# Swapping the side that carries the stride: activations that reorder tokens write SBUF in order and read PSUM strided

## The chip, the cores and the metric

The kernel runs on one core of a Trainium2 chip. The metric is device time in microseconds (us). A time is the median of several executions; different calls may run on different chips, so each comparison below is made with executions of the kernel before on the same chip, and a ratio compares the fast runs of the two kernels from the same rounds, as the measuring program worked it out. That is not quite the ratio of the medians quoted beside it. Profiles are single executions. Their span is about 2 us shorter than the device time of the same execution.

Engines in the profile: PE is the matrix engine (PEld its weight loads), ACT is ScalarE, DVE is VectorE, POOL is GpSimd, SP is SyncE.

## The reference

Two layers follow one another. The first is attention over 4 batches, 8 heads, 768 tokens and head size 64. A query sees the first 8 keys ("global") and the last 96 ("local"), with a bias that falls linearly with distance. The second takes the 3072 token rows of 512 values, sends each to one of 8 experts (top 1), or skips it, and adds the result:

```python
def _attn_ref(q, k, v, n_global, n_local):          # (4, 8, 768, 64), 8, 96
    scores = scale * np.matmul(q, k.transpose(0, 1, 3, 2))
    ...                                             # keep = is_global | is_local, plus bias
    a = np.exp(scores - max);  a = a / a.sum()
    return np.matmul(a, v)

def _moe_ref(x, w_skip, w_gate, w1, w2):            # x: (3072, 512)
    do_compute = x @ w_skip > 0
    e_idx = np.argmax(x[do_compute] @ w_gate, axis=1)
    ...
        h = np.maximum(xc[mask] @ w1[e], 0.0)
        y[mask] = gate_w[mask, None] * (h @ w2[e])
    out[do_compute] = xc + y
```

## The kernel before

Attention runs over 16 head pairs (a batch and two heads). q and k are loaded with eight neighbouring tokens in one SBUF partition: token `8p + r` sits in partition `p` (0 to 95) at place `r` (0 to 7). Transposing such a tile gives tokens in the order `(r, p)`. The kernel wants them back in the order `(p, r)`, which is the natural one, so the ScalarE instruction that moves a result from PSUM to SBUF also reorders it. In the kernel before, that instruction reads PSUM in order and writes SBUF with the stride: neighbouring elements of the stream land 8 bf16, that is 16 bytes, apart.

```python
# R = 8, P = 96, S = 768, W = 224
# transposes(n, 1): keys, PSUM (bf16) -> kt
kt = t_pool.tile([128, S], BF16, tag="kt", name="kt")
nc.scalar.activation(out=kt[:, :].rearrange("a (p r) -> a r p", r=R), in_=ps[:, :, :],
                     func=ACT.Copy)

# global_scores(b): scores against the global keys, PSUM (fp32) -> g_sb
nc.scalar.activation(
    out=g_sb[:, u * (S // 2):(u + 1) * (S // 2)].rearrange("a (p r) -> a r p", r=R),
    in_=gp[:, :, :], func=ACT.Exp, bias=gbias[:, 0:1], scale=scale)

# scores(n, g): local scores of two key tiles and two heads, PSUM (fp32) -> a
sc = ps_sc.tile([128, 2, 512], FP32, tag="sc", name="sc")
...                                        # matmuls write sc[:, hh, kk*W : ...] in order (r, p)
nc.scalar.activation(
    out=a[:, :, :].rearrange("a h (k p r) -> a h k r p", k=2, r=R),
    in_=sc[:, :, 0:2 * W].rearrange("a h (k r p) -> a h k r p", k=2, r=R),
    func=ACT.Exp, scale=scale)
...                                        # the last of three groups: two smaller activations
nc.vector.tensor_tensor(out=a[:, :, 0:wid], in0=a[:, :, 0:wid], in1=m[:, :, 0:wid], op=ALU.mult)
```

The loads of q, k and v are issued by GpSimd, and so are the small copies `kg` of the first keys of each head, which the global scores need:

```python
def load_v(b, ones=True):
    vb = v_pool.tile([128, T, H, D1], BF16, tag="vb", name="vb")
    for t in range(T):
        nc.gpsimd.dma_start(out=vb[:, t, :, 0:D], in_=v_r[b, t])
    nc.gpsimd.memset(vb[:, :, :, D:D1], 1.0)       # a column of ones beside v
    vbs[b] = vb

def keys_global(n):
    ...
        nc.gpsimd.tensor_copy(out=kg[b % 2][...], in_=kts[n][..., 0:KG])
```

After attention come the last gate, then a gather of each expert's tokens, the late weights (three of eight experts; the other five are loaded during attention), the experts' matmuls and the scatter of their results.

The softmax here doesn't subtract the row's maximum and nothing guards it: scores larger than these inputs give would overflow.

## Time and profile before

| | before |
|---|---|
| time, median of 3 (later 4) executions | 416.79 us (416.69) |
| ScalarE busy | 282.1 us, 68% of the span |
| matmul busy | 176.9 us, 43% |
| VectorE busy | 105.0 us, 25% |
| issue of the experts' first gather, start of the tail | 312.2 us |

From the page of the kernel before: the span, and each engine's busy us, share of the span and number of instructions.

```profile
span 414.9 us, 4722 instructions
...
PE 176.9 (43%) x1869; PEld 127.0 (31%) x1877; DVE 105.0 (25%) x311; ACT 282.1 (68%) x144; POOL 122.5 (30%) x183
...
```

The trace lacks eight matmul records: PE shows 1869 instructions here and 1877 in the other full traces.

The busy-by-stretch view cuts the run into stages; shown are the loop over the 16 head pairs and the tail. Its columns are the stretch, its length, each engine's busy us with its number of instructions, the granted clock of PE, the packet time of the DMA engines as a share of 16 of them (it can exceed 1) and GB/s.

```profile
...
46.00:297.00 251.00, 98.64 (x1209) 72.68 (x1208) 66.93 (x196) 219.91 (x89) 44.15 (x81) 0.81 0.52 76
312.00:415.00 103.00, 64.36 (x441) 43.03 (x449) 17.70 (x29) 19.02 (x32) 60.56 (x62) 0.81 0.61 144
...
```

In the loop, 46 to 297 us, ScalarE is busy 219.9 of 251 us. A head pair takes 251 / 16 = 15.7 us. In the tail it is busy 19 of 103. So only a saving in the loop and the start can pay through ScalarE.

Which instructions are they? The groups by form, ScalarE only (busy us, then mean ns of one):

```profile
...
L286 ACT ACTIVATE a<-sc 128x896 bf16<-128x896 f32 x32 | 133.9, 4436 | 4.6 <-PE sc L281 4.6
L245 ACT ACTIVATE kt<-tr 128x768 bf16<-128x768 bf16 x16 | 61.7, 3858 | 0.9 <-PE tr L237 0.9
L293 ACT ACTIVATE a<-sc 128x448 bf16<-128x448 f32 x16 | 37.1, 2316 | 0.0
L293 ACT ACTIVATE a<-sc 128x256 bf16<-128x256 f32 x16 | 26.2, 1640 | 0.0
L580 ACT ACTIVATE ht<-hps 128x512 bf16<-128x512 f32 x32 | 19.0, 597 | 64.9 <-PE hps L577 64.9
L264 ACT ACTIVATE g_sb<-gp,gbias 128x384 bf16<-128x384 f32 x8 | 14.7, 2081 | 16.0 <-PE gp L261 16.0
...
```

The first, second, third, fourth and sixth of these lines are the five forms that reorder. Together they record 133.9 + 61.7 + 37.1 + 26.2 + 14.7 = 273.6 us. The fifth, `ht`, does not reorder: 512 elements in 597 ns. An 896-element reorder takes 4436 ns, 7.4 times as long for 1.75 times the elements. Records of neighbouring instructions overlap a little; the chain of waits gives the net pace:

```profile
...
12.09 8.09 ACT a L286 x2
...
```

Two of them back to back take 8.09 us, which is 4.5 ns per element.

### The profile page before, as it was taken

Reading aid. Unit: us, or ns where it says so; the run is one execution under the profiler, and the core shown is the slowest. Engines: PE = TensorE matmul, PEld = TensorE weight load, DVE = VectorE, ACT = ScalarE, POOL = GpSimd, SP = SyncE. Lnnn points to the kernel's source line nnn. Section 1 sums busy time; section 2 is a strip of 40 time slices with the busy share of each in tenths; the row PEclk is TensorE's granted clock in tenths of the full one; section 3 lists DMA queues with packets and bytes.
Section 4 is the critical chain, followed back from the end, with each engine's and each line's share of the span. In section 5 each row is a group of like instructions: output and inputs, shape, how many; then the busy total and the mean of one; then the engine's idle time right before and its main releaser. Section 6 shows DMA issues by size and latency. Waiting matters only on the chain.

```text
span 414.9 us, 4722 instructions
## 1 busy us (share of the span) xinstructions
PE 176.9 (43%) x1869; PEld 127.0 (31%) x1877; DVE 105.0 (25%) x311; ACT 282.1 (68%) x144; POOL 122.5 (30%) x183
## 2 busy tenths in 40 slices
PE   1201643243344332424335150534533898399700
PEld 1101332232133332312324140323522575176400
DVE  5112122213111133241212233113761120232200
ACT  7999799999799996949999785898010232033200
POOL 8240642115101241010520000000007545477770
PEclk9999999999999999999555555656555899699965
DMA  8950792209402192040499997000204999544430
GB/s 117 125 76 2 92 63 38 38 2 114 114 2 38 17 98 39 0 114 2 68 203 212 212 212 183 0 2 0 77 0 88 231 230 199 173 130 136 128 96 15
DMA packets 50520, 38.24 MB, mean 92 GB/s; under 512 B 30276, under 2 KB 39492, under 8 KB 50496
## 3 DMA queue, kind: packets, MB, share of 16 engines
q0 software_dynamic: 45568, 34.62, 52.5%
q1 hardware_dynamic: 4928, 3.30, 2.8%
q8 instruction: 16, 0.26, 0.2%
q14 instruction: 8, 0.07, 0.1%
HBM read 54.68 MB, written 13.63 MB: 165 GB/s over the span
## 4 chain that ended last, share of the span: by engine, by line
ACT 43%; issue 21%; PE 13%; DMA 9%; DVE 9%; POOL 3%; POOLq 0%; ACTq 0%; DVEq 0%
ACT a L286 14%; ACT kt L245 12%; ACT a L293 12%; PE yps L584 4%; PE hps L577 3%; DMA w<-in_moe_w_dram 3%; DMA xg<-x_rows,src 3%; DMA out_dram<-y,rows 3%; ACT xts L360 2%; ACT g_sb L264 2%; POOL xg L545 1%; DVE xb L330 1%; PE gp L261 1%; PE sc L281 1%; ACT mask L161 1%
## 5 line engine op out<-in xcount | busy, mean ns | idle before, releaser
L286 ACT ACTIVATE a<-sc 128x896 bf16<-128x896 f32 x32 | 133.9, 4436 | 4.6 <-PE sc L281 4.6
L299 DVE TENSOR_TENSOR a<-a,mask 128x896 bf16<-128x896 bf16 (+1 forms) x48 | 28.7, 597 | 193.5 <-ACT a L286 106.0
L580 ACT ACTIVATE ht<-hps 128x512 bf16<-128x512 f32 x32 | 19.0, 597 | 64.9 <-PE hps L577 64.9
L245 ACT ACTIVATE kt<-tr 128x768 bf16<-128x768 bf16 x16 | 61.7, 3858 | 0.9 <-PE tr L237 0.9
L281 PE MATMUL sc<-qt,kt 64*128 64x224 bf16 x192 | 24.6, 354 | 81.3 <-ACT a L286 45.8
L293 ACT ACTIVATE a<-sc 128x448 bf16<-128x448 f32 (+1 forms) x32 | 55.1, 1978 | 0.0
L253 POOL COPY kg<-kt 64x16 bf16<-64x16 bf16 x32 | 6.1, 192 | 158.0 <-ACT kt L245 157.2
L545 POOL DMA_INDIRECT xg<-x_rows,src x16 | 15.7, 980 | 73.8 <-DVE gate L537 60.1
L281 PEld LDWEIGHTS <-kt 64*128 64x128 bf16 x192 | 9.4, 107 | 88.1 <-issue 72.6
L584 PE MATMUL yps<-w,ht 128*128 128x512 bf16 x120 | 29.2, 394 | 8.0 <-DVE y L589 7.6
L577 PE MATMUL hps<-xt,w 128*128 128x256 bf16 x256 | 31.4, 284 | 0.0
L237 PE MATMUL tr<-ident,qr 96*64 96x96 bf16 x256 | 13.6, 280 | 35.6 <-ACT kt L245 34.5
L554 POOL DMA_INDIRECT out_dram<-xb,skip_k x24 | 24.1, 1004 | 13.2 <-DMA w<-in_moe_w_dram 6.5
L577 PEld LDWEIGHTS <-w 128*128 128x128 bf16 x256 | 25.8, 102 | 4.1
L317 PE MATMUL av<-vb,a 128*128 128x65 bf16 x192 | 26.4, 243 | 0.0
L589 DVE SCALAR_TENSOR_TENSOR y<-yps,gate,xg 128x512 f32<-128x512 f32 x16 | 11.9, 750 | 54.4 <-PE yps L584 29.0
L264 ACT ACTIVATE g_sb<-gp,gbias 128x384 bf16<-128x384 f32 x8 | 14.7, 2081 | 16.0 <-PE gp L261 16.0
L324 PE MATMUL av<-vb,a 128*96 128x65 bf16 x160 | 25.0, 263 | 0.0
L317 PEld LDWEIGHTS <-a 128*128 128x128 bf16 x192 | 24.1, 150 | 0.0
L237 PEld LDWEIGHTS <-qr 96*64 96x64 bf16 x256 | 11.6, 163 | 36.3 <-issue 34.2
L324 PEld LDWEIGHTS <-a 128*96 128x96 bf16 x160 | 22.5, 180 | 0.0
L94 POOL DMA_DIRECT2D vb<-in_v_dram x24 | 21.3, 914 | 1.4 <-DMA kr<-in_k_dram 0.9
(115 smaller groups left out, 274.3 us busy)
## 6 DMA issues: line engine op xcount, KB each, us to landing
w<-in_moe_w_dram POOLq DMA_DIRECT2D x16, 1024.0 KB, 19.6
kr<-in_k_dram POOLq DMA_DIRECT2D x16, 192.0 KB, 3.4
qr<-in_q_dram POOLq DMA_DIRECT2D x16, 192.0 KB, 4.0
vb<-in_v_dram POOLq DMA_DIRECT2D x24, 128.0 KB, 5.3
x_rows<-xb SPq DMA_DIRECT2D x4, 768.0 KB, 3.7
out_dram<-xb,skip_k POOLq DMA_INDIRECT x24, 2.6
xg<-x_rows,src POOLq DMA_INDIRECT x16, 11.5
out_dram<-y,rows POOLq DMA_INDIRECT x16, 2.7
```

The lines of the kernel that those rows point to most:

```text
L237: nc.tensor.transpose(out=ps[hh * D:(hh + 1) * D, r, :], in_=raw[:, hh, r * D:(r + 1) * D], identity=ident[0:P, 0:P])
L245: nc.scalar.activation(out=kt[:, :].rearrange("a (p r) -> a r p", r=R), in_=ps[:, :, :], func=ACT.Copy)
L264: nc.scalar.activation(out=g_sb[:, u * (S // 2):(u + 1) * (S // 2)].rearrange("a (p r) -> a r p", r=R), in_=gp[:, :, :], func=ACT.Exp, bia ...
L281: nc.tensor.matmul(out=sc[:, hh, kk * W:kk * W + R * wp].rearrange("a (r p) -> a r p", r=R), lhsT=kt[rows, t * 128:(t + 1) * 128], rhs=qt[ ...
L286: nc.scalar.activation(out=a[:, :, :].rearrange("a h (k p r) -> a h k r p", k=2, r=R), in_=sc[:, :, 0:2 * W].rearrange("a h (k r p) -> a h ...
L293: nc.scalar.activation(out=a[:, :, lo:lo + R * wp].rearrange("a h (p r) -> a h r p", r=R), in_=sc[:, :, lo:lo + R * wp].rearrange("a h (r ...
L299: nc.vector.tensor_tensor(out=a[:, :, 0:wid], in0=a[:, :, 0:wid], in1=m[:, :, 0:wid], op=ALU.mult)
L317: nc.tensor.matmul(out=av[:, jj, hh, :], lhsT=a_sbs[n, t // 2][:, hh, (t % 2) * W:(t % 2) * W + 128], rhs=vb[:, t, h, :], start=False, sto ...
L324: nc.tensor.matmul(out=av[0:NL, jj, hh, :], lhsT=a_sbs[n, p // 2][:, hh, c:c + NL], rhs=vb[:, p, h, :], start=False, stop=(jj == 2 and hh ...
L554: put(nc.gpsimd.indirect_dma_start(out=out[:, :], out_offset=bass.IndirectOffsetOnAxis(ap=skip_k[:, t:t + 1], axis=0), in_=xbs[t // T][:, ...
L577: nc.tensor.matmul(out=hps[:, j, :], lhsT=w1_sb[e][:, dc, c2 * 256 + j:(c2 + 1) * 256:2], rhs=xt[:, dc, :], start=(dc == 0), stop=(dc == D ...
L584: nc.tensor.matmul(out=yps[:, :], lhsT=ht[:, f // 2, f % 2, c * 128:(c + 1) * 128], rhs=w2_sb[e][:, f // 2, (f % 2) * DM:(f % 2 + 1) * DM] ...
```

## The change

The intent: take the stride off the write and put it on the read. The writes of `kt`, `g_sb` and `a` become contiguous, and PSUM is read with steps of 112 bytes (`sc`; 64 in its smallest form) or 192 bytes (`kt`, `g_sb`). To make the read of the large score tile expressible, its PSUM layout goes from `[2, 512]` to `[2, 2, 256]`, so that head and key tile lie at one common step.

```diff
-            nc.scalar.activation(out=kt[:, :].rearrange("a (p r) -> a r p", r=R), in_=ps[:, :, :],
+            nc.scalar.activation(out=kt[:, :].rearrange("a (p r) -> a p r", r=R),
+                                 in_=ps[:, :, :].rearrange("a r p -> a p r"),
                                  func=ACT.Copy)
...
-                out=g_sb[:, u * (S // 2):(u + 1) * (S // 2)].rearrange("a (p r) -> a r p", r=R),
-                in_=gp[:, :, :], func=ACT.Exp, bias=gbias[:, 0:1], scale=scale)
+                out=g_sb[:, u * (S // 2):(u + 1) * (S // 2)].rearrange("a (p r) -> a p r", r=R),
+                in_=gp[:, :, :].rearrange("a r p -> a p r"), func=ACT.Exp, bias=gbias[:, 0:1], scale=scale)
...
-        sc = ps_sc.tile([128, 2, 512], FP32, tag="sc", name="sc")
+        sc = ps_sc.tile([128, 2, 2, 256], FP32, tag="sc", name="sc")
...
-                out=a[:, :, :].rearrange("a h (k p r) -> a h k r p", k=2, r=R),
-                in_=sc[:, :, 0:2 * W].rearrange("a h (k r p) -> a h k r p", k=2, r=R),
+                out=a[:, :, :].rearrange("a h (k p r) -> a h k p r", k=2, r=R),
+                in_=sc[:, :, :, 0:W].rearrange("a h k (r p) -> a h k p r", r=R),
...                                   # the same for the two smaller activations of the last group
```

No instruction is added, removed or moved; each engine's order is the same in both builds.

More of the change, by code (lines that the diff above doesn't have):

```diff
@@ L281, in scores @@
                 nc.tensor.matmul(
-                    out=sc[:, hh, kk * W:kk * W + R * wp].rearrange("a (r p) -> a r p", r=R),
+                    out=sc[:, hh, kk, 0:R * wp].rearrange("a (r p) -> a r p", r=R),
                     lhsT=kt[rows, t * 128:(t + 1) * 128],
@@ L291, in scores @@
         else:
-            for lo, wp in ((0, WP), (W, TP)):
+            for kk, wp in ((0, WP), (1, TP)):
+                lo = kk * W
                 nc.scalar.activation(
-                    out=a[:, :, lo:lo + R * wp].rearrange("a h (p r) -> a h r p", r=R),
-                    in_=sc[:, :, lo:lo + R * wp].rearrange("a h (r p) -> a h r p", r=R),
+                    out=a[:, :, lo:lo + R * wp].rearrange("a h (p r) -> a h p r", r=R),
+                    in_=sc[:, :, kk, 0:R * wp].rearrange("a h (r p) -> a h p r", r=R),
                     func=ACT.Exp, scale=scale)
```

## The prediction

> **What bounds the kernel now.** The page gives ScalarE 282.1 us of a 414.9 us span (68%), matmuls 176.9, VectorE 105.0. The busy-by-stretch view shows ScalarE nearly full from 25 to 270 us (27.0 of 27 us in 48-75, 40.0 of 40 in 190-230), with matmuls 11 to 19 us of each 40. So attention (the first 290 us or so) is bound by ScalarE. The rest (last gate, gathers, experts) is a tail; its chain shows late weights, gathers and PE.
>
> **What the change touches.** Five forms that reorder tokens while evacuating PSUM (groups by form): scores 896 elements, 32 times, 4436 ns; scores 448 and 256, 16 times each, 2316 and 1640 ns; kt 768, 16 times, 3858 ns; g_sb 384, 8 times, 2081 ns. In sum 273.6 us.  Back to back, two 896s take 8.09 us in the chain: 4.5 ns an element. The same engine evacuates in order at a fifth of that: xts (1024 bf16) 1307 ns alone, 0.85 us of the chain; the experts' ht (512 fp32) 597 ns. So the stride costs about 3.6 ns an element, near 200 us in all. The write now steps 16 bytes per bf16 element. The Trainium skill ("SBUF — State Buffer", Specifications) gives SBUF 16-byte lines and says at least two hits per line are needed for full bandwidth; 4.5 against 0.83 ns agrees that something here is heavily penalised.
>
> **After.** Writes in order; PSUM reads step 112 bytes (scores) or 192 (kt, g_sb). Instructions keep their number and order (I compared the builds). Whether ScalarE reads PSUM cheaply at such a stride no row here shows. The skill ("PSUM — Partial Sum Buffer", Specifications) gives 8-byte lines and says non-contiguous patterns slow matmuls, so a penalty is possible. Weak evidence against a large one on VectorE: strided 6-element PSUM reads (154 ns and 190 ns) cost no more than in-order SBUF ones (172, 192). My guess: 0.8 to 1.7 ns an element, so 896 elements take 0.95 to 1.7 us.
>
> **Critical path.** ScalarE would fall from about 16.5 us per head pair to 4 to 7. The gain stops at the next limit. PE's own work per pair, summed from the timeline of 127-137 us, is about 6.5 us; VectorE has about 5.4; two PSUM buffers shared by transposes and logits, and PE's in-order waits for the gate's VectorE work (31 and 14 us in the waits), add to it. I estimate 7.5 to 8.5 us per pair, 16 pairs, instead of 15.6. Start of the loop moves from 46 to about 22 us (then bound by q, k, v loads). Attention then ends near 150 to 160 us, not 290; the tail of 125 us stays. The early weights (10 MB at about 212 GB/s, 50 us) come from pair 8 on and should just be in time. Sum: about 280 us.
>
> **What would show it.** 896-element scores at 0.9 to 1.8 us; kt below 1.6 us; ScalarE busy 85 to 150 us in all; PE waiting less on ScalarE and attention bounded by PE and VectorE round trips; tail from the last gate still 120 to 130 us; DMA share up in the first 150 us.
>
> **What would make it wrong.** PSUM strided reads as dear as the strided writes (896 elements at 4 us): no gain, about 415 us. Reads at three cycles (2.5 ns): ScalarE stays the limit at 10 us a pair, about 315 us. Loads unable to feed a loop twice as fast, or early weights late into the experts, would add 10 to 30 us.
>
> Predicted 280 us, 80% range 257 to 332; faster by over 2% 0.90, within 2% 0.06, slower 0.04.

## The result, and the profile after

| | before | after |
|---|---|---|
| time, median | 416.69 us (415.14 to 416.87, 4 runs) | 260.12 us (259.15 to 262.22, 4 runs) |
| ratio | | 0.6254, 95% interval 0.6213 to 0.6296 |
| ScalarE busy | 282.1 us | 91.1 us |
| matmul busy | 176.9 us | 152.4 us |
| first gather issued | 312.2 us | 157.2 us |
| from the first gather to the end of the span | 102.7 us | 103.0 us |

The last two rows locate the gain. All of it, 155.0 us, came before the first gather; the tail is unchanged. (The span is 414.9 us before and 260.2 us after.) The issue of the first gather in the chain of the kernel before, then of the changed one:

```profile
...
312.22 1.06 POOL xg L545
...
```

```profile
...
157.21 1.06 POOL xg L547
...
```

From the page of the changed kernel, the same two lines (its eight further instructions are the matmul records that the trace before lacks):

```profile
span 260.2 us, 4730 instructions
...
PE 152.4 (59%) x1877; PEld 106.7 (41%) x1877; DVE 104.2 (40%) x311; ACT 91.1 (35%) x144; POOL 123.5 (47%) x183
...
```

Groups by form, ScalarE only, changed kernel:

```profile
...
L287 ACT ACTIVATE a<-sc 128x896 bf16<-128x896 f32 x32 | 28.9, 923 | 9.0 <-PE sc L282 8.2 <-DVE a L301 0.7
L582 ACT ACTIVATE ht<-hps 128x512 bf16<-128x512 f32 x32 | 19.0, 597 | 66.0 <-PE hps L579 66.0
L245 ACT ACTIVATE kt<-tr 128x768 bf16<-128x768 bf16 x16 | 13.0, 814 | 0.9 <-PE tr L237 0.9
...
L295 ACT ACTIVATE a<-sc 128x448 bf16<-128x448 f32 x16 | 8.9, 555 | 0.0
L295 ACT ACTIVATE a<-sc 128x256 bf16<-128x256 f32 x16 | 6.5, 407 | 0.0
L265 ACT ACTIVATE g_sb<-gp,gbias 128x384 bf16<-128x384 f32 x8 | 4.6, 581 | 48.1 <-PE gp L262 48.1
...
```

The five forms now record 28.9 + 13.0 + 8.9 + 6.5 + 4.6 = 61.9 us instead of 273.6. The difference between the 896 and the 448 form, (923 - 555) / 448, is 0.82 ns per element: with a 112-byte step on the PSUM read this is the full pace of the engine. The Trainium skill ("ScalarE: Activation LUTs", section "What ACT_TABLE_LOAD costs") gives 186 ns + 0.833 ns per element for an ACTIVATE with immediate scale and bias, and 280 ns with a bias from memory. As estimates from that page's figures, the 896, `kt` and `g_sb` forms (the last with bias) would take 932, 826 and 600 ns; the trace has 923, 814 and 581. So a strided read of PSUM costs ScalarE nothing that these rows show.

The busy-by-stretch view of the changed kernel, with stretches chosen for its own stages (the first four pairs, a stall, the other twelve pairs, the tail):

```profile
...
22.00:47.00 25.00, 17.42 (x296) 11.58 (x296) 13.79 (x34) 13.85 (x22) 17.81 (x33) 1.00 1.03 96
47.00:67.00 20.00, 1.34 (x3) 0.30 (x3) 1.43 (x4) 0.00 (x0) 10.96 (x21) 0.52 1.35 138
67.00:141.00 74.00, 54.72 (x910) 40.01 (x910) 50.34 (x158) 43.03 (x66) 22.47 (x44) 0.78 0.97 156
...
157.00:260.00 103.00, 65.24 (x449) 43.59 (x449) 17.69 (x29) 19.03 (x32) 60.58 (x62) 0.81 0.64 149
...
```

The second line is new. From 47 to 67 us PE ran three matmuls and ScalarE nothing. The timelines of GpSimd and of PE around it (start us, us, instruction, and in brackets the idle time before it and what ended it):

```profile
...
52.21 3.54 POOL L94 DMA_DIRECT2D vb<-in_v_dram  x4
57.43 1.82 POOL L94 DMA_DIRECT2D vb<-in_v_dram  x2 [1.68 <-DMA kr<-in_k_dram]
66.20 0.31 POOL L95 MEMSET vb<- 128x48 bf16 x1 [6.95 <-DMA vb<-in_v_dram]
66.57 0.44 POOL L254 COPY kg<-kt 64x16 bf16<-64x16 bf16 x2
...
```

```profile
...
67.07 1.14 PE L262 MATMUL gp<-qt,kg 128*128 128x384 bf16 x3 [15.49 <-POOL kg L254]
```

PE waits 15.49 us for the copy `kg`. The copy is queued on GpSimd behind the memset that writes the ones of v (L95), and the memset waits for the loads of v of batch 2, which is first used four pairs later, by the ninth pair. After that stall 12 pairs run in 74 us, 6.2 us each. In this stretch no engine is full: PE 54.7, VectorE 50.3, ScalarE 43.0 of 74 us.

### The profile page after: what moved, and what is told of

Its sections match the earlier page's. It is cut to its first block, busy times and chain, and to the rows that moved or that the text cites. A ratio compares the mean times of both kernels' runs of the same rounds, so it can differ in the third digit from the quotient of the medians.

```text
span 260.2 us, 4730 instructions
## 1 busy us (share of the span) xinstructions
PE 152.4 (59%) x1877; PEld 106.7 (41%) x1877; DVE 104.2 (40%) x311; ACT 91.1 (35%) x144; POOL 123.5 (47%) x183
## 4 chain that ended last, share of the span: by engine, by line
DMA 35%; PE 21%; POOL 14%; DVE 10%; ACT 8%; issue 7%; POOLq 0%; ACTq 0%; DVEq 0%
DMA vb<-in_v_dram 9%; PE yps L586 7%; DMA x_rows<-xb 6%; PE hps L579 5%; DMA xg<-x_rows,src 5%; DMA w<-in_moe_w_dram 5%; DMA out_dram<-y,rows 5%; DMA kr<-in_k_dram 3%; DMA qr<-in_q_dram 3%; ACT a L287 3%; PE gp L262 3%; ACT a L295 2%; DVE xb L332 2%; POOL xg L547 2%; ACT xts L362 2%
## 5 line engine op out<-in xcount | busy, mean ns | idle before, releaser
L287 ACT ACTIVATE a<-sc 128x896 bf16<-128x896 f32 x32 | 28.9, 923 | 9.0 <-PE sc L282 8.2
L262 PE MATMUL gp<-qt,kg 128*128 128x384 bf16 x32 | 11.9, 513 | 29.9 <-POOL kg L254 29.9
L586 PEld LDWEIGHTS <-ht 128*128 128x128 bf16 x128 | 12.8, 100 | 22.5 <-issue 9.9
L265 ACT ACTIVATE g_sb<-gp,gbias 128x384 bf16<-128x384 f32 x8 | 4.6, 581 | 48.1 <-PE gp L262 48.1
L282 PE MATMUL sc<-qt,kt 64*128 64x224 bf16 x192 | 19.8, 296 | 2.8 <-DVE qt L241 1.3
L319 PE MATMUL av<-vb,a 128*128 128x65 bf16 x192 | 19.1, 207 | 0.0
L262 PEld LDWEIGHTS <-kg 128*128 128x128 bf16 x32 | 4.0, 135 | 35.5 <-POOL kg L254 32.4
L332 DVE TENSOR_TENSOR xb<-av,rc 128x384 bf16<-128x384 f32 x32 | 17.8, 558 | 1.1
L326 PE MATMUL av<-vb,a 128*96 128x65 bf16 x160 | 18.3, 219 | 0.0
L594 POOL DMA_INDIRECT out_dram<-y,rows x16 | 15.9, 995 | 4.9 <-issue 3.7
L319 PEld LDWEIGHTS <-a 128*128 128x128 bf16 x192 | 17.0, 117 | 0.0
L326 PEld LDWEIGHTS <-a 128*96 128x96 bf16 x160 | 15.6, 138 | 0.0
## 6 DMA issues: line engine op xcount, KB each, us to landing
x_rows<-xb SPq DMA_DIRECT2D x4, 768.0 KB, 11.4
```

The source lines that it names most:

```text
L262: nc.tensor.matmul(out=gp[:, :, :], lhsT=kg[b % 2][:, hp, :], rhs=qts[b * HP + hp][:, :, u * (P // 2):(u + 1) * (P // 2)], start=(hp == 0) ...
L282: nc.tensor.matmul(out=sc[:, hh, kk, 0:R * wp].rearrange("a (r p) -> a r p", r=R), lhsT=kt[rows, t * 128:(t + 1) * 128], rhs=qt[rows, :, t ...
L287: nc.scalar.activation(out=a[:, :, :].rearrange("a h (k p r) -> a h k p r", k=2, r=R), in_=sc[:, :, :, 0:W].rearrange("a h k (r p) -> a h ...
L319: nc.tensor.matmul(out=av[:, jj, hh, :], lhsT=a_sbs[n, t // 2][:, hh, (t % 2) * W:(t % 2) * W + 128], rhs=vb[:, t, h, :], start=False, sto ...
L326: nc.tensor.matmul(out=av[0:NL, jj, hh, :], lhsT=a_sbs[n, p // 2][:, hh, c:c + NL], rhs=vb[:, p, h, :], start=False, stop=(jj == 2 and hh ...
L332: nc.vector.tensor_tensor(out=xb[:, 3 * u:3 * u + 3, 2 * hp * D:(2 * hp + 2) * D].rearrange("p j (h d) -> p j h d", h=2), in0=av[:, :, :, ...
```

## The experiments

The runs went to several chips; the kernel before took 417.1 us on one (as at first) and 424.7 to 426.8 us on the others. On a slower chip the loop's times agree and the tail is longer. For the changed kernel the first gather came at 157.2 us on the first chip, 157.1 us on a slower one; the tail was 103.0 and 109.6 us. That is why the issue of the first gather serves below as the end of attention. The two probes and the no-mask run were executed once each; only the durations of single instructions and the first gather are read from them.

The questions were two. First, what exactly made the old writes dear: a mere non-unit step, each opened line of SBUF, or something narrower? Second, what limits the changed kernel, and did it swallow part of the gain: ScalarE's busy time fell by 191 us, the way to the first gather by 155?

### A probe of access patterns

Edit: the changed kernel with one extra copy per head pair, from the transposed keys in PSUM (or from `kt`) into a scratch tile, each with another pattern. The results stay right. `ps` is the transposed tile in PSUM, `pin` the same read in order, `jb` the scratch tile.

```diff
             kts[n] = kt
+            if n == 0:      # in order
+                nc.scalar.activation(out=jb[:, 0:768], in_=pin, func=ACT.Copy)
+            ...             # n == 1: read strided; n == 2..6: write steps of 4, 8, 16, 32, 64 bytes
+            elif n == 7:    # runs of two neighbours, 16 bytes from run to run
+                nc.scalar.activation(out=jb[:, 0:768].rearrange("a (p r s) -> a r p s", r=4, s=2),
+                                     in_=ps.rearrange("a (r s) p -> a r p s", s=2), func=ACT.Copy)
+            ...             # fp32 outputs, strided SBUF read, VectorE
```

> The changed kernel with one extra ScalarE copy of a transposed kt tile into a scratch tile for each of 16 head pairs, each with another access pattern (one on VectorE), and four early experts instead of five to make room; the output stays right, the total time means nothing. Theory W (it is the write to SBUF: each write that opens a new 16-byte line costs): in-order 768 elements about 0.82 us; strided PSUM read with in-order write the same; writes with step 4 and 8 bytes near in-order speed (0.8 to 1.7 ns an element); step 16, 32 and 64 bytes all about 4.5 ns; runs of two elements at 16 bytes about half of that per element or in order; fp32 with 16-byte step as dear as bf16 with 16-byte step. Rival N (any write that is not unit-step is slow, whatever the line): step 4 and 8 bytes already about 4.5 ns. Rival S (partial word writes of bf16 are slow, not the line): fp32 with 16-byte step near 0.83 ns. A strided read of SBUF with an in-order write stays near 0.83 ns if only writes pay; VectorE writing with 16-byte step, 640 elements, below 1.0 us if the penalty is ScalarE's alone, 3 us if it is SBUF's.

Measured, from the view of the scratch tile's instructions (durations ns as min/median/max, one instruction each). In order: L256 in order; L258 PSUM read strided, write in order; L260, L262, L264, L266, L268 bf16 writes with steps of 4, 8, 16, 32 and 64 bytes; L270 runs of two bf16 every 16 bytes; L274 fp32 written in order; L276 and L278 fp32 writes with steps of 8 and 16 bytes; L282 SBUF read with a 16-byte step, write in order; L286 VectorE writing with a 16-byte step.

```profile
...
L256 ACT ACTIVATE junk<-tr x1: 789/789/789, 11.1 to 11.1; 128x768 bf16<-128x768 bf16 x1
L258 ACT ACTIVATE junk<-tr x1: 858/858/858, 14.8 to 14.8; 128x768 bf16<-128x768 bf16 x1
L260 ACT ACTIVATE junk<-tr x1: 1070/1070/1070, 18.9 to 18.9; 128x768 bf16<-128x768 bf16 x1
L262 ACT ACTIVATE junk<-tr x1: 1864/1864/1864, 21.1 to 21.1; 128x768 bf16<-128x768 bf16 x1
L264 ACT ACTIVATE junk<-tr x1: 3029/3029/3029, 33.5 to 33.5; 128x640 bf16<-128x640 bf16 x1
L266 ACT ACTIVATE junk<-tr x1: 1599/1599/1599, 39.4 to 39.4; 128x320 bf16<-128x320 bf16 x1
L268 ACT ACTIVATE junk<-tr x1: 868/868/868, 44.5 to 44.5; 128x160 bf16<-128x160 bf16 x1
L270 ACT ACTIVATE junk<-tr x1: 861/861/861, 48.2 to 48.2; 128x768 bf16<-128x768 bf16 x1
...
L274 ACT ACTIVATE junk<-tr x1: 898/898/898, 76.5 to 76.5; 128x768 f32<-128x768 bf16 x1
L276 ACT ACTIVATE junk<-tr x1: 1059/1059/1059, 81.1 to 81.1; 128x768 f32<-128x768 bf16 x1
L278 ACT ACTIVATE junk<-tr x1: 1297/1297/1297, 90.9 to 90.9; 128x640 f32<-128x640 bf16 x1
...
L282 ACT ACTIVATE junk<-kt x1: 1611/1611/1611, 108.4 to 108.4; 128x768 bf16<-128x768 bf16 x1
...
L286 DVE COPY junk<-tr x1: 2998/2998/2998, 125.8 to 125.8; 128x640 bf16<-128x640 bf16 x1
...
```

What follows:

- A strided PSUM read costs next to nothing: 858 against 789 ns. A strided read of SBUF is not free: 1611 ns.
- The dear side is the write into SBUF, and it is not ScalarE's own doing: VectorE takes 2998 ns for the same 640 elements where ScalarE takes 3029.
- Rival N falls in part: steps of 4 and 8 bytes cost 1070 and 1864 ns, not the 4.5 ns per element of 16 bytes.
- Theory W falls as stated. It expected fp32 to be as dear as bf16, and at most 1.7 ns an element at a step of 8 bytes. But fp32 at a 16-byte step took 1297 ns where bf16 took 3029, and the step of 8 bytes took 2.4 ns an element (1864 / 768). For runs of two it had left open half the cost or full pace; they ran at full pace (861 ns, though a new line was opened for every two elements, 384 in all).
- Rival S is half right: the half word is what is dear, yet a lone fp32 per line is not quite free (1297 ns for 640 elements, against 898 ns for 768 in order).

Reading the numbers per 16-byte line makes them simple. I take 0.17 us off each as the fixed part (the in-order 640 elements of the next run took 697 ns, less 640 x 0.82). With one lone bf16 per word, a line cost 4.7 ns when it got four of them (900 / 192), 4.4 when two (1694 / 384), 4.5 when one (2859 / 640), and 4.5 and 4.4 at steps of 32 and 64 bytes. Where one whole 4-byte word was written, a line cost 1.8 ns (fp32 at 16 bytes, 1127 / 640; pairs of bf16, 691 / 384, of which two elements at 0.82 ns are already 1.6). With two whole words it cost 2.3 ns (fp32 at 8 bytes, 889 / 384). The new theory, H: a line of SBUF that is written with half words costs about 4.5 ns; one that gets one whole word costs about 1.8 ns.

### The probe again, with pairs that do not fill a word

One instruction each is thin, and "whole word" could also mean "any two neighbours in one line". The second probe has 640 elements in each pattern, each twice, and adds pairs shifted by one bf16, so that both elements lie in one line but in two words. `pp` is `pin` as pairs.

```diff
+            elif n % 8 == 3:   # aligned pairs
+                nc.scalar.activation(out=jb[:, 0:2560].rearrange("a (p s) -> a p s", s=8)[:, :, 0:2], in_=pp, ...)
+            elif n % 8 == 4:   # shifted pairs
+                nc.scalar.activation(out=jb[:, 0:2560].rearrange("a (p s) -> a p s", s=8)[:, :, 1:3], in_=pp, ...)
```

> Second probe, each pattern twice (two head pairs), 640 elements each, read in order from PSUM, written to a scratch tile; four early experts, result stays right, total time means nothing. Theory H (whole 4-byte words in a 16-byte line are cheap, half words cost the line about 4.5 ns): in order 0.7 us; bf16 step 8 bytes 1.5 to 1.7; step 16 bytes 3.0; aligned pairs at 16 bytes 0.7 to 0.8; pairs that straddle two words (shifted by one bf16) dear, 1.4 to 1.7 us for 320 lines; fp32 at 16 bytes 1.3; VectorE in order 0.7 to 0.8 and aligned pairs near that. Rival R (any run of two neighbours in one line is enough, whatever the word): shifted pairs as cheap as aligned ones, 0.7 to 0.8 us.

Measured, same view. L256 in order, L258 step 8 bytes, L260 step 16, L262 aligned pairs, L264 shifted pairs, L266 fp32 at 16 bytes, L268 VectorE in order, L270 VectorE aligned pairs.

```profile
...
L256 ACT ACTIVATE junk<-tr x2: 682/697/712, 11.1 to 71.4; 128x640 bf16<-128x640 bf16 x2
L258 ACT ACTIVATE junk<-tr x2: 1637/1675/1713, 14.8 to 75.8; 128x640 bf16<-128x640 bf16 x2
L260 ACT ACTIVATE junk<-tr x2: 3057/3129/3201, 19.2 to 81.1; 128x640 bf16<-128x640 bf16 x2
L262 ACT ACTIVATE junk<-tr x2: 737/762/788, 22.8 to 93.0; 128x640 bf16<-128x640 bf16 x2
L264 ACT ACTIVATE junk<-tr x2: 1583/1590/1597, 33.9 to 105.4; 128x640 bf16<-128x640 bf16 x2
L266 ACT ACTIVATE junk<-tr x2: 1394/1397/1400, 38.3 to 110.7; 128x640 f32<-128x640 bf16 x2
L268 DVE COPY junk<-tr x2: 478/482/485, 44.1 to 117.1; 128x640 bf16<-128x640 bf16 x2
L270 DVE COPY junk<-tr x2: 715/722/730, 48.4 to 124.8; 128x640 bf16<-128x640 bf16 x2
...
```

Shifted pairs take 1590 ns against 762 for aligned ones, with the same number of elements, runs and lines. Rival R falls and H stands: (1590 - 170) / 320 = 4.4 ns a line against (762 - 170) / 320 = 1.9. The Trainium skill ("SBUF — State Buffer", Specifications) says that at least two hits per 16-byte line give full bandwidth. The runs agree for aligned pairs and differ for two other cases with two hits: a step of 8 bytes (1675 ns) and shifted pairs (1590 ns). What inside the memory makes half words dear, no run shows. On VectorE the in-order copy took 482 ns, faster than the 0.7 to 0.8 us that I expected, and aligned pairs took 722 ns, half as much again: pairs are nearly free on ScalarE only (762 against 697 ns).

### H in the kernel itself: still strided, but in pairs

If H holds, the kernel before needs no in-order write at all for `kt` and `g_sb`: pairs are enough.

```diff
-            nc.scalar.activation(out=kt[:, :].rearrange("a (p r) -> a r p", r=R), in_=ps[:, :, :], ...)
+            nc.scalar.activation(out=kt[:, :].rearrange("a (p r s) -> a r p s", r=R // 2, s=2),
+                                 in_=ps[:, :, :].rearrange("a (r s) p -> a r p s", s=2), ...)
```

(and the same for `g_sb`; the scores stay as before.)

> The kernel before, but kt and g_sb are written in runs of two neighbouring bf16 (4 bytes) each 16 bytes, still strided; the scores stay as they were. Theory H (a 16-byte line of SBUF written with half words only costs about 4.5 ns, whole 4-byte words cost at most 1.8 ns a line, so pairs run at full rate): kt falls from 3858 to 0.8-0.9 us and g_sb from 2081 to about 0.6 us, as in the changed kernel; ScalarE loses about 60 us, all of it on the path, so the time falls by 50 to 62 us to about 0.86 of before. Rival L (each newly opened line costs 4.5 ns whatever is written into it): kt 1.9 to 2.2 us, time falls by about 30 us, to 0.93.

Measured: 375.37 us against 424.79 us for the kernel before on that chip, ratio 0.8838 (0.8823 to 0.8853), a gain of 49.4 us. It is just under the range for H and far over what L allowed. `g_sb` fell from 2081 to 602 ns. `kt` records 1153 ns, over the 0.8 to 0.9 us that I expected; the timeline of ScalarE shows why:

```profile
...
103.09 8.47 ACT L287 ACTIVATE a<-sc 128x896 bf16<-128x896 f32 x2
111.05 1.20 ACT L245 ACTIVATE kt<-tr 128x768 bf16<-128x768 bf16 x1
```

The two score activations end at 103.09 + 8.47 = 111.56 us, and `kt`, recorded from 111.05, ends at 112.25: its record overlaps theirs by 0.51 us, and it adds 0.69 us. ScalarE's busy time fell by 52.4 us (282.1 to 229.7) and the first gather came 49.2 us earlier (263.0 us). So in the kernel before a microsecond of ScalarE was nearly a microsecond of time.

### The same microseconds in the changed kernel

The mirror image: the changed kernel with `kt` alone written as before (the first hunk of the diff undone).

> The changed kernel with kt alone written as before, with 16-byte steps. ScalarE gets back 16 x 3.04 = 48.7 us. If ScalarE were still the limit of attention, the time would rise by 45 to 50 us over the changed kernel; my theory is that it is not (loads, PE and VectorE round trips are), so most is hidden: rise of 5 to 25 us.

The changed kernel unaltered, as a base on the same chip:

> The changed kernel unaltered, on the chip of this call, as the base of the three runs beside it: ratio to the kernel before near 0.625, as at first, if the chip doesn't matter; the first call's chip gave 424.7 us for the kernel before, 2% over the chip of the first result.

Measured: the unaltered one 269.08 us, ratio to before 0.6334 (0.6301 to 0.6368); with `kt` as before 290.08 us, ratio 0.6815. ScalarE's busy time rose by 42.5 us (133.5 against 91.0), the time by 21.0, the first gather from 157.1 to 178.4 us. Half was hidden. So in the changed kernel ScalarE is no longer the one limit, and a microsecond of it is worth about half.

### What the new limit is: the ones written first

Edit, on the changed kernel:

```diff
+        nc.gpsimd.memset(vb[:, :, :, D:D1], 1.0)
         for t in range(T):
             nc.gpsimd.dma_start(out=vb[:, t, :, 0:D], in_=v_r[b, t])
-        nc.gpsimd.memset(vb[:, :, :, D:D1], 1.0)
```

> The changed kernel with the ones column of v written before its loads are issued, not after. Theory Q (the new limit in the first 90 us is GpSimd's in-order queue: the memset waits for the v loads, and the key copies and the next loads behind it wait too): GpSimd's 26.9 us of waiting for v loads go, matmuls' 29.9 us of waiting for the key copies fall below 12, and the time falls by 10 to 25 us to 235 to 250. Rival D (the loads of q, k and v themselves are as slow as the engines need them, the memset only sits where the wait shows): the waits move to other lines and the time stays within 4 us of 260.

The same edit on the kernel before, as a control:

> The kernel before with the same edit. ScalarE is the limit there, so both theories expect the same time as before, 415 to 418 us; if it falls by over 2%, the vb wait was a cost before the change too.

And the changed kernel, with the old order of memset and loads, but with v loaded for the first batch only (wrong result):

```diff
+        if b > 0:
+            vbs[b] = vbs[0]
+            return
         vb = v_pool.tile([128, T, H, D1], BF16, tag="vb", name="vb")
```

> The changed kernel with v loaded for the first batch only and used for all (wrong result on purpose): takes away both the memset's waits and 18 of 24 v loads. Theory Q: hardly faster than with the ones written first (within 6 us of that run). Rival D: much faster than it, by 12 us or more, because the traffic itself is gone; total 225 to 240 us.

Measured, all on one chip:

| run | time, us | ratio to before | first gather, us |
|---|---|---|---|
| ones first | 247.29 | 0.5833 (0.5794 to 0.5872) | 134.2 |
| kernel before, ones first | 424.75 | 1.0001 (0.9957 to 1.0044) | 312.1 |
| one v load only, wrong | 245.76 | 0.5801 (0.577 to 0.5831) | 134.1 |

The ones first bring the first gather 23 us forward. Taking away 18 of 24 loads of v altogether brings it no further (134.1), so the traffic of v as such was not the limit: Theory Q holds, D falls. The control shows that the same order cost the kernel before nothing: there ScalarE was later anyway.

Both were run again side by side:

> The changed kernel again, as the base of the run beside it in the same call, since its ratio to before was 0.625 on the first chip and 0.633 in a later call: 0.625 to 0.635.

> The ones-first kernel beside the changed kernel on one chip. By the first gather of the experts (157.2 us against 134.2 us in the profiles) 23 us should be saved; I expect 16 to 23 us of the time, 0.91 to 0.94 of the changed kernel. If it is under 10 us, the tail gives back more than half of it.

Measured: the changed kernel 258.89 us, ratio 0.6205 (0.619 to 0.6219), just under what was expected; ones first 240.50 us, ratio 0.5731 (0.5702 to 0.576). That is 18.4 us, 0.924 of the changed kernel. (One of the four ones-first executions, 241.74 us, counts as slow and is left out of the ratio; the median of the other three is 239.85 us, 19.0 us less than the changed kernel.) The first gather moved from 156.1 to 136.3 us and the tails are equal (102.9 and 102.8 us). The waits, first in the changed kernel (its first profile), then with ones first (us in total, times, longest):

```profile
...
PE gp L262 <- POOL kg L254: 29.9, 8, 15.5
...
POOL vb L95 <- DMA vb<-in_v_dram: 26.9, 4, 8.4
...
```

```profile
...
PE gp L262 <- POOL kg L254: 9.0, 3, 7.0
...
```

GpSimd's wait for v is gone from the list, and PE's wait for `kg` fell from 29.9 to 9.0 us. The busy-by-stretch view of the ones-first kernel shows work where the changed kernel stood still:

```profile
...
47.00:67.00 20.00, 16.44 (x298) 12.14 (x298) 13.86 (x44) 14.26 (x21) 10.88 (x19) 0.84 1.62 134
...
```

From 47 to 67 us PE now runs 298 matmuls instead of 3. This version beats both kernels.

### Two attempts to go further, both misses

First, is VectorE the pace of a head pair in the ones-first kernel? Edit: no mask product for the first score tile of each pair (wrong).

```diff
-        nc.vector.tensor_tensor(out=a[:, :, 0:wid], ...)
+        if g != 0:
+            nc.vector.tensor_tensor(out=a[:, :, 0:wid], ...)
```

> The ones-first kernel without the mask product of the first score tile of each head pair (wrong result on purpose): takes 16 x 0.63 = 10 us from VectorE. Theory V (after the loads are out of the way, VectorE's in-order work sets the pace of a head pair): the first gather of the experts comes 6 to 12 us earlier than the 134.2 us of the ones-first kernel. Rival P (PE's in-order stream sets it): earlier by under 3 us.

The first gather came at 135.3 us, no earlier than 134.2 (on another chip). Theory V falls. The rival, PE's in-order stream, is not thereby shown; it only survived. (The whole time of this run, 340.72 us, says nothing: the wrong rows were routed so unevenly that a second round of experts ran, with 32 gathers instead of 16.)

Second, does the tail wait because gathers queue behind weight loads? Edit, on the ones-first kernel:

```diff
         for e in range(E):
             gather(e, src)
-            if first and e % 2 == 1 and EARLY + e // 2 < E:
-                load_weights(EARLY + e // 2, wlate)
+        for e in range(EARLY, E):
+            if first:
+                load_weights(e, wlate)
```

> The ones of v first, and in the expert stage all 16 gathers are issued before the late weights, not interleaved with them. Theory T (the tail waits since gathers queue behind 2 MB weight loads on the same DMA engines): the waits for xg (12 us) and the DMA pieces of the chain (weights 18 us, gathers 14 us) shrink and the time falls by 8 to 25 us below the ones-first kernel (0.583 of before). Rival B (the tail is bound by its bytes or by GpSimd's issue of about 1 us per indirect transfer): within 4 us of it.

Measured: 253.73 us, ratio 0.5976 (0.5939 to 0.6013), which is worse than the ones-first kernel (0.5833). Attention ended as before, first gather at 135.4 us. From there to the end of the span it took 115.9 us, against 109.6 us for the unaltered changed kernel on the same chip and 110.6 us for the ones-first kernel on another. So the interleaved order is the better one, and what bounds the tail stays open.

## Why the prediction was right or wrong

The time, 260.12 us, lies in the range (257 to 332), near its lower end, and 20 us under the middle. That it came no further off is partly luck: two errors of opposite sign, a loop put 29 us too long and a stall of 20 us left out, offset each other. Point by point:

- **ScalarE bounds attention, by the five reordering forms.** Right. The pairs run shows it from the other side: 52.4 us off ScalarE gave 49.2 us of attention.
- **The stride costs about 3.6 ns an element on the write, and a strided read is cheap.** Right in size: 0.82 ns an element after, at the low end of the guess of 0.8 to 1.7. The reason given, lines of 16 bytes that need two hits, was incomplete. What costs is a line written with half words, about 4.5 ns, whether it gets one, two or four of them. That a strided read would be cheap was a guess with weak evidence, called so; it held.
- **The start of the loop moves from 46 to about 22 us.** Right: the first matmul of the global scores moved from 46.5 to 22.6 us.
- **7.5 to 8.5 us per pair from the next limits.** The mechanism was right (round trips among PE, VectorE and ScalarE, no engine full), the size was off. Outside the stall a pair took 6.2 us; in the ones-first kernel, which has no such stall, 6.3 us (from 18.4 us, the first matmul of the global scores, to 118.5 us, the last write of token rows, over 16 pairs). This is the term that was mis-sized: 16 pairs times about 1.8 us is 29 us too much. One cause is visible. I took PE's 6.5 us per pair from the trace of before, where PE worked at a slower pace: in the loop 1209 matmuls kept it busy for 98.6 us before and 73.5 us after (17.42 + 1.34 + 54.72). Sixteen transposes before, then in the changed kernel:

```profile
...
126.88 0.85 PE L237 MATMUL tr<-ident,qr 96*64 96x96 bf16 x16 [5.64 <-ACT kt L245]
```

```profile
...
73.24 0.53 PE L237 MATMUL tr<-ident,qr 96*64 96x96 bf16 x16
...
```

  The Trainium skill ("TensorE: Matmul & The Clock Gate", section "What's actually happening") describes this: PE starts throttled and is released by sustained activity. The traces agree, 0.85 against 0.53 us for the same work: a PE that waits less also works faster. In the changed kernel sixteen transposes take 0.85 us where the view prints a granted clock of about a half (0.52 from 67 to 72 us) and 0.53 us where it prints 1.00 (72 to 80 us). The 1.00 that it prints for the kernel before from 120 to 160 us is wrong: its trace has no clock record before 188 us (nor has that of the changed kernel before 34 us), the transposes take 0.85 us there, and the control of before (ones first), whose record covers that stretch, has 0.50. How many of the 29 us are due to this pace, no run separates.
- **Loads might be unable to feed a loop twice as fast, 10 to 30 us.** It was named as a risk and left out of the sum, and it happened: 20 us, from 47 to 67 us. The cause was other than the one named. Not the rate of the loads, but the order in GpSimd's queue; the ones-first run took it away with the same bytes. The sum of the miss: the loop 29 us too long, the stall 20 us left out, the tail 6 us too long (125 against 118.9), and about 5 us of rounding up, together 20 us.
- **Early weights just in time.** Nearly so. The last write of the token rows took 15.05 us in the chain, and the median of the four such writes rose from 3.7 to 11.4 us. The early weights were moving at the same time and are the likely reason; no run separates them. Little was lost by it: in the changed kernel the write ended at 156.34 us and the last step of the gate, which the gathers need too, at 156.18; in the ones-first kernel at 135.47 and 135.52.
- **The tail of about 125 us stays.** Right in kind: 102.7 and 103.0 us from the first gather; from the last write of token rows 118.3 (414.9 - 296.6) and 118.9 us (260.2 - 141.3).
- **Where did the rest of ScalarE's 191 us go?** 155 came out as time. Of the other 36, the queue order accounts for 20 to 23, shown by the ones-first runs. The remaining 13 or so fit the round trips; that is argued, not shown.

## What to carry to other kernels

When an instruction must reorder on its way from PSUM to SBUF, put the stride on the PSUM read (112 and 192 bytes here) and let the SBUF write run in order; where that cannot be expressed, write whole aligned 4-byte words, which cost ScalarE here nearly the same as in-order writes for runs of two bf16. After removing a large cost from the busiest engine, look for in-order queues where something that is needed later stands in front of something needed now: such an order is free as long as another engine is later still, and shows only afterwards. And read the pace of the next engine with care, since one that used to wait may work faster once it is kept busy.

## What the Trainium skill lacked or had wrong

- "SBUF — State Buffer", Specifications: two hits in a 16-byte line are said to give full bandwidth. Measured for writes: enough only if they fill an aligned 4-byte word (762 ns for 640 bf16 in aligned pairs; 1590 ns for pairs that straddle two words; 1675 ns at a step of 8 bytes; 697 ns in order).
- Same page: no size is given for the penalty. Measured: 4.4 to 4.7 ns for a line written with half words by ScalarE, about 1.8 to 1.9 ns for one that gets one whole word; VectorE pays alike for half words (2998 ns for 640 bf16 at a 16-byte step, 482 ns in order) and more for aligned pairs (722 ns). A strided read of SBUF at 16 bytes by ScalarE cost 1611 ns for 768 bf16.
- "PSUM — Partial Sum Buffer", Specifications: the 8-byte line is given with a warning for matmuls only. Nothing is said of what a stride costs ScalarE's reads; here steps of 112 and 192 bytes cost next to nothing (923 ns for 896 fp32, 858 against 789 ns for 768 bf16).
- "ScalarE: Activation LUTs", section "What ACT_TABLE_LOAD costs": back-to-back ACTIVATEs are said to overlap by about 93 ns. After one that writes with half words the overlap was 0.51 us, so that one `kt` recorded 1.20 us and added 0.69.
